# One kernel of a recurrence and a gated layer: constants from one ramp, and a new written order with other banks, queues and engines of copies

## The chip, the core and the metric

The kernel runs on one core of one Trainium2 chip. A core has TensorE (PE in the profile; its weight loads are PEld), VectorE (DVE), ScalarE (ACT) and GpSimd (POOL), which compute, and SyncE (SP), which here only issues transfers. ScalarE and GpSimd can issue transfers too, between their computing instructions. All transfers run on the core's 16 DMA engines. The metric is the device time of one execution in microseconds.

## The reference

A recurrence over 768 steps for 4 batches and 8 heads of 48 channels, and behind it a layer on its 3072 rows of 384:

```python
state = np.zeros((B, H, D, D))
for t in range(S):
    cur = np.einsum('bhd,bhe->bhde', u[None] * kt, vt)
    y[:, :, t] = np.einsum('bhd,bhde->bhe', rt, state + cur)
    state = wt[:, :, :, None] * state + np.einsum('bhd,bhe->bhde', kt, vt)
...
h = x @ w_in                                  # 384 x 1024
sm = e / (np.sum(e, axis=-1, keepdims=True) + 1e-09)      # e = exp(h - max h)
solu = h * sm
ln = (solu - mu) / np.sqrt(var + 1e-06) * g_ln
return (ln @ w_out).astype(np.float32)        # 1024 x 384
```

r, k, v, w, u are the attention inputs (w lies between 0.8 and 0.95), all float32; x is y with its heads side by side.

## The kernel before

The 768 steps are cut into 6 chunks of 128, and a chunk of one batch is a *unit*: 24 units, number 4 times the chunk plus the batch. A unit goes through these stages; the short names are those of the code's table `stages`, and a number behind one is the unit.

- LW, LK, LR, LV load w, k, r and v (192 KB each, into rings of seven buffers).
- lw takes the logarithm of w (ScalarE); cum sums it over the steps with two triangular matrices, `uti_neg` and `uts` (TensorE, 384 columns each); ex is the exponential of the sums, in place in PSUM (ScalarE); kp multiplies by k and r (VectorE) and thereby empties two PSUM banks.
- krk and krr transpose k and r on TensorE, kr copies the result out of PSUM (ScalarE or VectorE). For some units kt does all this with one transposing transfer by SP.
- M is the matrix of scores, m its masked copy (VectorE multiplies with a triangular 0/1 matrix, `keep`).
- p and q are products k r u (GpSimd), dg their sum (VectorE), dv that sum times v (GpSimd): the bonus of the current step. vb is v in bf16 (ScalarE or GpSimd).
- Y is the attention output; y copies it out. Either VectorE adds dv in that copy (the word Y ends in n), or TensorE adds it first with an identity matmul of 384 columns (i) and ScalarE copies.
- S, et, st carry the state on; et is an exponential of 8 columns, st VectorE's update. S uses `halves` and `off_blocks` to set the entries between different heads to exp(-30000).
- X and xT transpose y; H is the product with w_in (24 matmuls of 128 columns into two banks); e its exponential, he the product h e (VectorE), hq its square; Oa and Ob are the two halves of the product with w_out (386 columns), together with one- and two-column matmuls that sum e, he and hq over the row. ea adds the two halves of e beforehand (GpSimd), so that four matmuls sum e and not eight.
- qm, lv, rs make the scale of the row from those sums (VectorE, ScalarE, ScalarE), o scales, out stores.

The softmax sum and the mean cancel out of the layer norm except for these sums, so that no row is divided before the end. Units 17 to 20 make H with rows as the output and turn he by a transfer (ht). Unit 23 is done in two halves (HA, HB and so on).

The weights are prepared once: LI loads w_in in three parts, wi casts them; LO loads w_out in two halves, gw multiplies its eight blocks by the gain, mn forms their column mean (TensorE), mc copies it (ScalarE), ce subtracts it from each block. hot is a number of matmuls of zeros. u and g are spread with us and gs.

The order is written out by hand as a text of words, `ORDER`. A word is a stage with its unit, and behind a point the PSUM bank, or the engine or queue: a for ScalarE, d VectorE, p GpSimd, g GpSimd's queue; a load or store with nothing there is issued by SP. Each engine executes its words strictly in this order (the class `InOrder`, through which every instruction goes: that is why nearly all rows of the profile carry line 86), and the transfers of SP and ScalarE are put in the order of the words too. So a transfer that ScalarE issues stands in its queue between two computing words, and a word that waits holds up all later words of its engine. The first lines, those around the first products with w_in, and the end:

```
hot10.0 LK3.a LW3 LR3.g LW0.a LR0.a lw3 cum3.0 hot2.2 LU0 LW2 LK0.a LG0 lw0 LR2.g cum0.2 ex3 us0.4 LV0.a LW4 LK2
lw2 lw4 kp3 gs0.5 ex0 LR4.g LK4 kp0 cum4.0 ih0 LV4.g ik0 LV2.g LV3.g LR6.g cum2.6 LW1.a uc0 p0 ex2 ex4 krk0.2 kp2
...
st2 Y4.i5 st3 X1.0 lw7 LW9 xT2.a et5 y3.a st4 y4.a lw8 LK8 m5.d mn0.2 X3.4 xT1.d q5 cum7.0 xT3.a st5 ex7 p7 X4.5
H0.6 lw10 mc0 ce7.p ce0.d e0 ce4.d LK10 ce6.d kp7 H1.3 LR8 ce2.d lw9 LW11 e1 he0 ce3.d LV11.g ce5.p H3.0 qh5
...
EB23 out19 DA23 Ob21 QA23.a DB23 qm21 Ob22 lv21 rs21 QB23.d o21.a qm22 out20 out21 lv22 rs22 o22.d out22 Oa23.5
Ob23 qm23 lv23 rs23 o23.a out23
```

The constants (`uti_neg`, `uts`, `ident_f`, `ident`, and later `halves`, `off_blocks`, `keep` by the words ih and ik) are made by GpSimd with memsets and affine selects, sixteen instructions in all.

Of the kernel before, what the change touches and what calls it, by code (L numbers as in the profile page):

```python
# [21 lines left out]
hot10.0 LK3.a LW3 LR3.g LW0.a LR0.a lw3 cum3.0 hot2.2 LU0 LW2 LK0.a LG0 lw0 LR2.g cum0.2 ex3 us0.4 LV0.a LW4 LK2  # L22
lw2 lw4 kp3 gs0.5 ex0 LR4.g LK4 kp0 cum4.0 ih0 LV4.g ik0 LV2.g LV3.g LR6.g cum2.6 LW1.a uc0 p0 ex2 ex4 krk0.2 kp2
krr0 krk3.4 LK1.a LW6 krk2.3 vb0.a krr2 LR5.g kr0.d kr2.a kp4 LK6 krr3 hot1.2 kr3.d M0.1 M3.3 m0.d LR1.a lw6 S0.0
LV1.a m3.d p2 q0 lw1 gc0 LW5 cum6.6 ex6 M2.1 cum1.4 krk4.3 LI0.a krr4 LK5 dg0 m2.d vb3.a kp6 vb2.a lw5 et0 ex1
st0 LO1 vb4.a kp1 cum5.6 hot1.0 q2 LV5.g p3 p1 dv0 ex5 krk1.4 q3 Y0.i5 q1 krr1 dg2 dv2 vb1.a krk6.0 S1.1 LO0.a
kp5 p5 p4 krr6 y0.a kr4.a dg3 krk5.5 dg1 dv1 q4 krr5 kr6.d kr1.a kr5.d et1 Y2.i6 hot1.0 y2.a vb5.a st1 LI2.a M1.2
S3.0 dv3 m1.d wi0.a M4.6 LW7 X0.1 xT0.d S2.5 gw7.a m4.d dg4 LV6.g et3 X2.4 p6 gw4.a LI1.a Y1.n1 LR7.g dv4 LR11.g
y1.d gw2.a gw5.a S4.2 LW10 M6.6 et2 et4 gw0.a S5.3 gw3.a LW8 wi2.p wi1.p gw1.a gw6.a LK7 Y3.i1 q6 m6.d M5.6 LR10
st2 Y4.i5 st3 X1.0 lw7 LW9 xT2.a et5 y3.a st4 y4.a lw8 LK8 m5.d mn0.2 X3.4 xT1.d q5 cum7.0 xT3.a st5 ex7 p7 X4.5  # L30
H0.6 lw10 mc0 ce7.p ce0.d e0 ce4.d LK10 ce6.d kp7 H1.3 LR8 ce2.d lw9 LW11 e1 he0 ce3.d LV11.g ce5.p H3.0 qh5
xT4.d ce1.d LK9 H2.6 hq0.a he1 e3 he3 LW12 e2 krk7.5 Oa0.2 he2 krr7 hq1.a cum10.3 LV8.g Ob0 ex10 Oa1.0 LR9 hq3.a
LV7 p8 cum8.6 LW13 Ob1 LW14 LK11 ex8 q7 vb6.p dg5 kr7.d kp10 lw11 qm0 Oa3.5 lv0 qm1 lv1 LV10.g p10 q8 rs0 M7.3
dg7 rs1 dv5 o0.a out0 vb7.p kp8 lw12 hq2.a Ob3 cum11.6 krk10.2 o1.d H4.0 m7.d Y5.n4 LR12.g dv7 Oa2.3 krr10 qm3
out1 p9 dg6 dg8 ex11 vb8.a dv6 q9 kp11 lv3 cum9.6 e4 rs3 Ob2 y5.d LV9 o3.a he4 ex9 kp9 lw14 kr10.a S7.5 LK12
Y6.n1 qm2 y6.d lv2 krk8.4 Y7.n0 krk11.6 krr8 y7.d S8.7 X5.2 et7 st7 krr11 lw13 rs2 LW17 o2.a et8 cum12.0 LR14.g
xT5.a ex12 q10 kr8.d S6.5 kr11.d hq4.a krk9.2 vb11.p out3 LK14 out2 M8.3 LK13 LR15.g LR17.g krr9 st8 kp12 LK17
et6 kr9.d H5.6 X6.0 m8.a M10.1 st6 e5 xT6.d M9.3 p11 Oa4.5 m10.d LW15 he5 q11 LR13.g X7.0 kt12 cum14.1 m9.a xT7.a
dv8 M11.3 ex14 m11.d sel8 Ob4 vb9.p kp14 LK15 hq5.a cum13.6 LW18 lw17 qm4 S11.0 ex13 Oa5.4 sel9 lv4 lw15 cum17.1
dg9 rs4 LR18.g kp13 Y8.n3 Ob5 ex17 cum15.6 y8.d dv9 o4.a Y9.n3 out4 LV12.g kp17 LV15.g et11 qm5 kt14 S9.5 st11  # L40
ex15 lv5 vb10.a y9.d H6.1 rs5 et9 LV14.g o5.a e6 st9 LV13.g kp15 p12 p13 dg11 he6 dg10 X8.3 X9.0 xT8.a H7.4 out5
q12 xT9.a e7 lw18 hq6.a H8.6 dv11 e8 M12.0 LV16.g he7 H9.2 m12.d LK18 Oa6.5 he8 dg12 e9 vb12.a S10.4 kt15 he9
hq7.a Ob6 hq8.a dv10 LW16 qm6 lv6 rs6 p14 LR16.g et10 Y11.n1 S12.0 et12 Oa7.6 o6.a LK16 y11.d lw16 Y10.n7 st10
Ob7 kt13 y10.d M14.3 st12 vb15.a LK20 M15.1 q13 vb13.a hq9.a qm7 m14.d m15.d lv7 dv12 rs7 Y12.n5 o7.a Oa8.0 y12.d
cum16.3 X11.7 Ob8 cum18.1 out6 p15 ex16 X12.5 xT11.d q14 q15 LR19.g qm8 kp16 vb16.a lv8 H11.6 rs8 o8.a ex18
xT12.d H12.4 LR20.g LW21 vb14.p dg13 LW19 dg15 e11 Oa9.0 p16 kp18 out7 e12 X10.1 dv15 he11 Ob9 xT10.a ea11.p he12
q16 lw21 hq11.a out8 qm9 lv9 M13.1 S15.3 et15 rs9 m13.d ea12.p cum21.4 ex21 o9.d H10.6 LK21 LR21 LW20 Oa11.0
LV18.g st15 kp21 lw19 cum19.1 e10 Ob11 Y15.n4 he10 hq12.a LK19 p18 kt16 S13.3 dv13 Y13.n5 S16.6 qm11 ex19 y15.d
# [52 lines left out]
def kernel(  # L101
# [14 lines left out]
    C = 128  # L116
# [551 lines left out]
```

## Time and profile before

| | |
|---|---|
| three runs | 150.04, 149.55, 146.75 us; median 149.55 |
| the profiled execution | 147.21 us, of which 143.9 are its span |
| mean granted TensorE clock | 0.975 of full speed |
| busy share of the span | PE 90%, VectorE 88%, ScalarE 83%, GpSimd 82% |
| read from HBM, written | 22.03 MB, 4.72 MB |

The page divides the span into 40 slices and gives each engine's busy share in tenths. Groups of instructions stand as line, engine, operation, output and inputs, shapes and count, then their busy time and the mean of one in ns, then the idle time ahead of them and what ended it. In rows in order of time the first number is the start, the second the length, both in us; in square brackets stands the idle time of the engine just before, with what ended it. The mean of a matmul is its way through the array; how fast matmuls follow one another is read from the difference of starts.

### The profile page before, as it was taken

How to read it: one execution, taken by the hardware profiler on the slowest of the kernel's cores; microseconds unless marked ns; L12 is line 12 of the kernel's file. 1: busy time of each engine (PE TensorE's matmuls, PEld its weight loads, DVE VectorE, ACT ScalarE, POOL GpSimd, SP SyncE). 2: the span in 40 equal slices, each digit the busy share in tenths (PEclk: the TensorE clock that was granted, in tenths of full speed). 3: DMA queues.
4: the chain of work that ended last, by engine and by line, in shares of the span. 5: the costliest groups of instructions: out<-in, count | busy, mean ns of one | idle time of the engine just before them, and what ended most of it. 6: DMA issues, size and time to landing. Idle time of an engine off the chain costs nothing.

```text
span 143.9 us, 4779 instructions
## 1 busy us (share of the span) xinstructions
PE 129.1 (90%) x1883; PEld 96.4 (67%) x1883; DVE 126.3 (88%) x218; ACT 119.0 (83%) x241; POOL 117.7 (82%) x151
## 2 busy tenths in 40 slices
PE   6958749869599999999999999999999999999980
PEld 2326418657586778868988787779787565776750
DVE  6028998995899999999999999999999999989760
ACT  3547786989769999999998999959997979967762
POOL 7999959999999989978999999989996997433000
PEclk9995986999999999999999999999999999999999
DMA  4999999999998799999999999999999979443312
GB/s 95 276 287 323 272 310 356 365 348 261 179 267 185 133 245 247 240 201 178 256 225 257 239 262 222 194 280 228 199 199 226 204 170 140 116 107 118 135 55 109
DMA packets 89927, 31.33 MB, mean 218 GB/s; under 512 B 83833, under 2 KB 87938, under 8 KB 89906
## 3 DMA queue, kind: packets, MB, share of 16 engines
q1 hardware_dynamic: 77474, 20.43, 66.2%
q0 software_dynamic: 2112, 6.49, 16.2%
q10 hardware_dynamic: 10320, 4.13, 10.2%
q8 instruction: 14, 0.23, 0.6%
q14 instruction: 7, 0.06, 0.1%
HBM read 22.03 MB, written 4.72 MB: 186 GB/s over the span
## 4 chain that ended last, share of the span: by engine, by line
PE 56%; DMA 20%; DVE 11%; ACT 7%; issue 3%; DVEq 0%; ACTq 0%
PE ps L86 56%; DMA w_in<-in_w_dram 6%; DMA v_in<-in_v_dram 5%; DMA wout_f<-in_moe_w_out_dram 4%; DMA kr_in<-in_k_dram 4%; DVE kp L86 3%; DVE he L86 2%; DVE m L86 2%; ACT w L86 1%; DVE w L86 1%; ACT ps L86 1%; ACT lw L86 1%; DVE dg L86 1%; ACT o L86 1%; DVE y L86 1%
## 5 line engine op out<-in xcount | busy, mean ns | idle before, releaser
L86 PE MATMUL ps<-w,he 128*128 128x386 bf16 x192 | 43.7, 324 | 0.1
L86 PE MATMUL ps<-xT,win_sb 128*128 128x128 bf16 x480 | 29.8, 219 | 1.7 <-DVE kp L86 1.5
L86 PEld LDWEIGHTS <-win_sb 128*128 128x128 bf16 x480 | 27.4, 98 | 3.1 <-DVE kp L86 1.7
L86 DVE TENSOR_TENSOR kp<-ps,kr_in 128x768 bf16<-128x768 f32 x24 | 22.8, 949 | 7.3 <-DMA kr_in<-in_r_dram 4.2
L86 DVE TENSOR_TENSOR m<-ps,keep 128x1024 bf16<-128x1024 f32 x22 | 26.4, 1213 | 0.0
L86 PE MATMUL ps<-one_col,hq 128*128 128x1 bf16 x160 | 26.1, 163 | 0.1
L86 POOL TENSOR_TENSOR p<-kr_in 128x384 bf16<-128x384 f32 x24 | 24.1, 1009 | 1.9 <-DMA kr_in<-in_r_dram 1.7
L86 POOL TENSOR_TENSOR dv<-vb,dg 128x384 bf16<-128x384 bf16 x24 | 20.0, 833 | 6.6 <-DVE dg L86 6.5
L86 DVE TENSOR_TENSOR he<-ps,e 128x1024 bf16<-128x1024 f32 (+1 forms) x21 | 24.1, 1163 | 0.8 <-ACT e L86 0.8
L86 ACT ACTIVATE e<-ps 128x1024 bf16<-128x1024 f32 (+1 forms) x25 | 24.3, 989 | 0.2
L86 ACT ACTIVATE hq<-he 128x1024 bf16<-128x1024 bf16 (+1 forms) x20 | 20.5, 1033 | 2.3 <-DVE he L86 2.3
L86 POOL TENSOR_TENSOR q<-p,u_bc 128x384 bf16<-128x384 bf16 x24 | 21.7, 916 | 0.4 <-DVE dg L86 0.2
L86 PEld LDWEIGHTS <-he 128*128 128x128 bf16 x192 | 18.2, 96 | 3.8
L86 ACT ACTIVATE ps<-ps 128x768 f32<-128x768 f32 x24 | 19.1, 800 | 1.0 <-PE ps L86 0.7
L86 PEld LDWEIGHTS <-hq 128*128 128x128 bf16 x160 | 13.7, 96 | 8.5 <-ACT hq L86 0.3
L86 ACT ACTIVATE lw<-w_in 128x384 bf16<-128x384 f32 x24 | 12.4, 522 | 6.8 <-DMA w_in<-in_w_dram 6.8
L86 POOL DMA_DIRECT2D v_in<-in_v_dram x17 | 15.5, 912 | 0.0
L86 PEld LDWEIGHTS <-kp 128*128 128x128 bf16 x176 | 12.3, 105 | 4.3 <-DVE kp L86 2.7
L86 POOL DMA_DIRECT2D kr_in<-in_r_dram x16 | 14.7, 921 | 0.0
L86 PEld LDWEIGHTS <-kr 64*128 64x128 bf16 (+1 forms) x272 | 10.4, 95 | 6.1 <-issue 2.5
L86 PE MATMUL ps<-signs,e 128*128 128x2 bf16 x88 | 14.5, 165 | 0.0
L86 POOL TENSOR_TENSOR ea<-e 128x512 bf16<-128x512 bf16 x9 | 10.4, 1154 | 5.0 <-ACT e L86 5.0
(94 smaller groups left out, 281.1 us busy)
## 6 DMA issues: line engine op xcount, KB each, us to landing
out_dram<-o SPq DMA_DIRECT2D x24, 192.0 KB, 3.3
w_in<-in_w_dram SPq DMA_DIRECT2D x22, 192.0 KB, 4.7
kr_in<-in_k_dram SPq DMA_DIRECT2D x21, 192.0 KB, 4.5
v_in<-in_v_dram POOLq DMA_DIRECT2D x17, 192.0 KB, 4.8
kr_in<-in_r_dram POOLq DMA_DIRECT2D x16, 192.0 KB, 4.7
win_f<-in_moe_w_in_dram ACTq DMA_DIRECT2D x3, 512.0 KB, 6.6
kr_in<-in_r_dram SPq DMA_DIRECT2D x6, 192.0 KB, 3.9
v_in<-in_v_dram SPq DMA_DIRECT2D x5, 192.0 KB, 6.1
```

What stands on the lines that cost most here:

```text
L86: made = make(*args, **kwargs)
```

## The change

Constants: GpSimd makes one ramp (column minus row) and VectorE compares it with zero for the triangles and the identity; `halves` and `off_blocks` are made by VectorE memsets, with the two rows that count at partitions 0 and 64 instead of 0 and 1. `keep` had the same entries as `uts`, which now masks the scores.

```diff
+    ramp = consts.tile([C, C], BF16)
+    pool.iota(ramp, pattern=[[1, C]], base=0, channel_multiplier=-1, allow_small_or_imprecise_dtypes=True)
     uti_neg = consts.tile([C, C], BF16)
-    pool.memset(uti_neg, -1.0)
-    pool.affine_select(out=uti_neg, in_=uti_neg, compare_op=ALU.is_ge, fill=0.0, base=0,
-                       pattern=[[1, C]], channel_multiplier=-1)
+    dve.tensor_scalar(out=uti_neg, in0=ramp, scalar1=0.0, scalar2=-1.0, op0=ALU.is_ge, op1=MULT)
     uts = consts.tile([C, C], BF16)
-    pool.memset(uts, 1.0)
...
+    dve.tensor_scalar(out=uts, in0=ramp, scalar1=0.0, scalar2=None, op0=ALU.is_gt)
...
+    dve.tensor_scalar(out=ident, in0=ramp, scalar1=0.0, scalar2=None, op0=ALU.is_equal)
...
+    for a in range(2):
+        row = slice(64 * a, 64 * a + 1)
+        dve.memset(halves[row, 64 * a:64 * a + 64], 1.0)
+        dve.memset(off_blocks[row, :, 1 - a:2 - a], -30000.0)
...
-                           in1=keep.unsqueeze(1).to_broadcast([C, H, C]))
+                           in1=uts.unsqueeze(1).to_broadcast([C, H, C]))
```

`ORDER` is replaced as a whole. The new lines in the places shown above:

```
LW3 LW0.a LR3.g LU0 LR0.a hot6.0 LW4 LG0 LK0.g LW2 hot1.0 hot7.0 LK3.g LK4 LR2.g hot4.1 lw3 LK2.g lw0 LW1.a
cum3.4 LW5 us0.1 LR4.g ex3 cum0.6 ex0 LV2.g gs0.0 lw4 LV0.a kp0 p0 uc0 LW6 gc0 hot1.0 LK1.g kp3 cum4.6 krk0.2 lw2
...
et5 y2.a p5 M6.2 st5 LV11 y3.a LK7.a m6.d LW10 gw6.a LV7.a X3.0 dv4 M5.6 gw5.a X1.4 X2.1 gw4.d q5 gw7.a S4.5 m5.d
Y4.i3 wi0.a wi1.p LV6 mn0.2 xT3.a xT2.d LW13 lw7 LW11.a LK10.g wi2.d et4 cum7.0 xT1.d mc0 H0.6 st4 LW8.g ex7
ce7.d LK11 LR10.g y4.a kp7 H1.4 e0 ce1.p ce3.d vb7.d lw10 LK8.a ce2.p H3.0 he0 LV8 e1 LK9.a p6 ce4.d hq0.a H2.6
...
out20 Oa22.6 QA23.a qm21 DB23 lv21 Oa23.0 rs21 o21.a QB23.d out21.a Ob22 Ob23 qm22 lv22 rs22 o22.a qm23 lv23
out22 rs23 o23.a out23.a
```

What the words add up to, where it differs:

| | before | after |
|---|---|---|
| loads of w, k, r, v by SP, ScalarE, GpSimd | 54, 9, 33 | 32, 31, 33 |
| loads of the weights by SP, ScalarE | 1, 4 | 2, 3 |
| stores by SP, ScalarE | 24, 0 | 17, 7 |
| copies of y by VectorE, ScalarE | 20, 4 | 14, 10 |
| copies of kr by VectorE, ScalarE; by transfer | 8, 4; 12 | 4, 7; 13 |
| casts of v by VectorE, ScalarE, GpSimd | 0, 15, 9 | 4, 9, 11 |
| copies of xT by VectorE, ScalarE | 11, 12 | 9, 14 |
| scalings o by VectorE, ScalarE | 6, 18 | 7, 17 |
| units with ea on GpSimd | 9 | 5 |
| casts of w_in by VectorE, ScalarE, GpSimd | 0, 1, 2 | 1, 1, 1 |
| gains of w_out by VectorE, ScalarE, GpSimd | 0, 8, 0 | 1, 6, 1 |
| centrings of w_out by VectorE, GpSimd | 6, 2 | 4, 4 |
| warm-up matmuls in all; ahead of the first cum | 15; 10 | 19; 18 |

The weights' loads come as LI0, LO1, LO0, LI2, LI1 before, and as LO0, LO1, LI2, LI1, LI0 after. Which loads go to which queue differs for more than half of the units; y moves to ScalarE for units 1, 5, 6, 8, 16 and 21, kr for units 3, 5 and 6, and unit 11's k and r are turned by a transfer. ea goes for units 10, 11, 13 and 14. v is cast by VectorE for units 0, 4, 7 and 8. Nearly every bank number differs.

More of the change, by code (lines that the diff above doesn't have):

```diff
@@ L5 @@
 from concourse import mybir
-from concourse.masks import make_identity
 from concourse._compat import with_exitstack
@@ L27 @@
[L27 to L36, printed above, removed]
@@ L206 @@
             dve.memset(kp_t[j][:, :, :, D:], 0.0)
+    ident = consts.tile([C, C], BF16)
+    dve.tensor_scalar(out=ident, in0=ramp, scalar1=0.0, scalar2=None, op0=ALU.is_equal)
+    ident_f = consts.tile([KF, KF], F32)
+    dve.tensor_scalar(out=ident_f, in0=ramp[:KF, :KF], scalar1=0.0, scalar2=None, op0=ALU.is_equal)
+    halves = consts.tile([C, C], BF16)
+    dve.memset(halves, 0.0)
+    off_blocks = consts.tile([C, HP, 2], BF16)
+    dve.memset(off_blocks, 0.0)
+    for a in range(2):
+        row = slice(64 * a, 64 * a + 1)
+        dve.memset(halves[row, 64 * a:64 * a + 64], 1.0)
+        dve.memset(off_blocks[row, :, 1 - a:2 - a], -30000.0)
     mean_w = consts.tile([128, 128], BF16)
@@ L296, in turn_g @@
         ps["g"] = bank([128, KF], F32, x, "g_ps")
-        pe.transpose(ps["g"], g_rows, ident_f[:KF, :KF])
+        pe.transpose(ps["g"], g_rows, ident_f)
     def copy_g(i, x):
```

97 lines of the change are left out of this document (37 added, 60 removed).

## The prediction

> **What bounds the kernel now.** I read the page first, then the busy time of each engine by stage, then the order of time around the two borders that the stages showed.
>
> ```profile
> span 143.9 us, 4779 instructions
> ...
> PE 129.1 (90%) x1883; PEld 96.4 (67%) x1883; DVE 126.3 (88%) x218; ACT 119.0 (83%) x241; POOL 117.7 (82%) x151
> ...
> PE   6958749869599999999999999999999999999980
> ...
> DVE  6028998995899999999999999999999999989760
> ```
>
> Two regimes stand in the slices of 3.6 us. From the twelfth slice on PE and DVE are both full. Before that PE has holes, and DVE has few after the third slice. The table by stage gives the borders; its columns are length, then busy time of PE, weight loads, DVE, ACT and POOL, then granted clock, DMA share, GB/s.
>
> ```profile
> 0.00:10.80 10.80, 7.78 (x23) 3.09 (x23) 3.13 (x24) 4.79 (x8) 9.53 (x27) 0.99 0.97 219
> 10.80:34.30 23.50, 18.14 (x249) 12.93 (x248) 22.17 (x31) 19.10 (x41) 21.71 (x25) 0.86 1.15 324
> 34.30:39.03 4.73, 3.21 (x54) 2.84 (x51) 2.60 (x6) 4.36 (x8) 4.71 (x7) 1.00 0.93 203
> 39.03:133.80 94.77, 94.26 (x1487) 73.63 (x1488) 93.77 (x149) 85.34 (x171) 81.71 (x95) 1.00 0.95 205
> 133.80:143.90 10.10, 5.74 (x77) 3.93 (x74) 4.60 (x10) 5.45 (x16) 0.00 (x0) 0.99 0.26 98
> ```
>
> The long stage, 94.77 us, is closed: PE is busy for 94.26 of it at full clock. A change there can win about 0.5 us unless it takes matmuls away. So gains must come from the 39 us ahead of it, where DVE (22.17 of 23.50) carries the chain, and from the 4.73 us between, where neither PE nor DVE is full. These rows, in order of time, are that border:
>
> ```profile
> 7.33 0.96 DVE L86 TENSOR_TENSOR kp<-ps,kr_in 128x768 bf16<-128x768 f32 x1 [4.23 <-DMA kr_in<-in_r_dram]
> ...
> 9.56 0.52 ACT L86 ACTIVATE lw<-w_in 128x384 bf16<-128x384 f32 x1 [1.96 <-DMA w_in<-in_w_dram]
> ...
> 10.82 0.96 DVE L86 TENSOR_TENSOR kp<-ps,kr_in 128x768 bf16<-128x768 f32 x1 [2.53 <-ACT ps L86]
> ...
> 32.62 2.03 POOL L86 CAST win_sb<-win_f 128x1024 bf16<-128x1024 f32 x2
> ...
> 34.49 3.02 PE L86 MATMUL ps<-xT,win_sb 128*128 128x128 bf16 x48
> ...
> 36.44 1.67 DVE L86 SCALAR_TENSOR_TENSOR w<-wout_f,gr,ps 128x384 bf16<-128x384 f32 x3 [2.13 <-ACT mean_sb L86]
> ...
> 38.02 0.95 DVE L86 TENSOR_TENSOR kp<-ps,kr_in 128x768 bf16<-128x768 f32 x1
> ...
> 39.03 3.15 PE L86 MATMUL ps<-xT,win_sb 128*128 128x128 bf16 x48 [1.52 <-DVE kp L86]
> ```
>
> H0 and H1 start at 34.49, when GpSimd has cast two thirds of w_in. H3 must wait for kp7 to empty its banks, kp7 stands behind three centrings of w_out, and those waited 2.13 us for ScalarE to copy the column mean.
>
> **The change, part by part.** *The start.* GpSimd's sixteen small constant instructions become one iota and ten short VectorE ones. In the trace of before VectorE's first real work is at 7.33, so those lie in its idle time; the cover is over 2 us deep. GpSimd's first load was at 2.69 and can now go up to 1.9 us earlier. Against that, 18 warm-up matmuls stand ahead of the first cumulation where 10 stood.
>
> ```profile
> 1.65 4.05 PE L86 MATMUL ps<-warm 128*128 128x512 bf16 x9
> ...
> 2.69 2.81 POOL L86 DMA_DIRECT2D kr_in<-in_r_dram  x3
> ...
> 6.13 1.06 PE L86 MATMUL ps<-warm 128*128 128x512 bf16 x2
> 6.38 0.80 ACT L86 ACTIVATE ps<-ps 128x768 f32<-128x768 f32 x1 [0.35 <-PE ps L86]
> ```
>
> Nine took 4.05 us, so eight more cost up to 3.6 us, and half of that once the clock is up (the 384-column matmuls further down pass in 0.16 us, where 512 columns take 0.45 here). Nearest to the mixture is 2.5 us: the first cumulation at about 8.0 instead of 5.5. Unit 3's exponential follows, then unit 0's (0.80 us each), since the wait at 9.56 for unit 4's w no longer stands between them. First kp at about 10.1, second at about 11.0, both done near 12.0; before, the second ended at 11.78. So the start gives +0.2 us (from -1.7, if the earlier loads carry the whole chain, to +1.5).
>
> *VectorE's chain to H0.* Durations, for the pieces that change engine:
>
> ```profile
> L86 DVE TENSOR_TENSOR y<-ps,dv 128x384 bf16<-128x384 f32 x20 | 10.9, 548 | 0.5 <-PE ps L86 0.4
> L86 DVE COPY kr<-ps 128x1024 bf16<-128x1024 bf16 x8 | 5.3, 680 | 0.6 <-PE ps L86 0.6
> L86 ACT COPY kr<-ps 128x1024 bf16<-128x1024 bf16 x4 | 4.0, 1016 | 0.9 <-PE ps L86 0.9
> L86 ACT CAST y<-ps 128x384 bf16<-128x384 f32 x4 | 1.9, 494 | 0.0
> L86 ACT CAST vb<-v_in 128x384 bf16<-128x384 f32 x15 | 7.4, 508 | 1.4 <-DMA v_in<-in_v_dram 1.4
> L86 POOL TENSOR_TENSOR ea<-e 128x512 bf16<-128x512 bf16 x9 | 10.4, 1154 | 5.0 <-ACT e L86 5.0
> L86 DVE SCALAR_TENSOR_TENSOR w<-wout_f,gr,ps 128x384 bf16<-128x384 f32 x6 | 3.5, 608 | 2.1 <-ACT mean_sb L86 2.1
> L86 POOL TENSOR_TENSOR w<-w,mean_sb 128x384 bf16<-128x384 bf16 x2 | 1.7, 838 | 0.0
> ```
>
> VectorE loses three kr copies (3 x 0.68) and one y (0.55): -2.6. It gains two casts of v, a gain of w_out and the cast of w_in's third part. None of these stands in the trace on VectorE; bounded by 0.35 and 0.68 for the small ones and by 0.7 and 1.2 for the 1024-wide one, I take 0.45 three times and 1.0: +2.4. Net -0.2. ScalarE gets three kr (3.0) and one y (0.5) and loses two casts of v (1.0) and two gains of w_out (1.2, if one is as long as a centring): +1.3, in a stage where it has 4.4 idle. GpSimd casts one part of w_in instead of two (-1.0), takes one gain (0.8, like its centring) and issues 14 loads ahead of H0 instead of 12 (2 x 0.94), against the constants that it no longer makes. The third w_in part now needs 1.0 us on three engines side by side, not 2.03 on one, so H0 hangs on VectorE's chain and on the mean product. One state update (st4, a 384-wide piece like y's 0.55) stands behind H0 now: 34.5 + 0.2 - 0.2 - 0.5 = 34.0.
>
> *The border.* Between the mean product and its copy ScalarE has an x copy, a logarithm and a short exponential, no longer an 0.8 us one; and VectorE has w_in's cast, two x copies and st4 to do in the 2.13 us in which it waited. Ahead of kp7 stands one centring, not three: 34.0 + 0.5 + 0.6 + 0.95 = 36.1. H3 then follows H1 directly, at 34.0 + 2.7 = 36.7 (two of the 24-matmul products, 1.36 us each by the spacing of 0.06 in the row below), not at 39.03: -2.3 us, the start and the chain included. That is the value I take; it is 0 if kp7 comes where it came, and -4.7 if the whole gap goes.
>
> *The long stage.* Spacing of PE's starts, in the thick of it:
>
> ```profile
> 60.77 0.17 PE L86 MATMUL ps<-signs,e 128*128 128x2 bf16 x1
> 60.80 0.16 PE L86 MATMUL ps<-one_col,hq 128*128 128x1 bf16 x1
> ...
> 63.55 0.32 PE L86 MATMUL ps<-st,ident 128*128 128x384 bf16 x1
> 63.71 0.33 PE L86 MATMUL ps<-vb,kp 128*128 128x96 bf16 x4
> ...
> 67.47 1.50 PE L86 MATMUL ps<-xT,win_sb 128*128 128x128 bf16 x24
> ```
>
> Five y copies of this stage go from VectorE to ScalarE, and the bonus term is then added by a 384-column matmul: 5 x 0.16 = +0.8. Four units lose GpSimd's sum of halves and need eight signed matmuls instead of four: 16 x 0.03 = +0.5. Unit 11's k and r are turned by a DMA: eight matmuls of 0.06 fewer, -0.5. PE: +0.8, all of it on the path. VectorE is relieved of about 3 us here (5 y and one kr are 3.4, two x copies go, a cast and an output scaling come), GpSimd of 4 x 1.15 less three casts; with PE full at 94.26 of 94.77 this can buy back up to 0.5, and I count 0.3.
>
> ScalarE is the doubtful one. Its work grows by 1.4 us (five y at 0.49, three casts of v at 0.51 fewer, two more x copies less one output scaling at about the same length). It had 13 DMA issues, all ahead of H0; now it has 41, of which some 24 lie in the long stage, each in its queue between two computing instructions.
>
> ```profile
> 16.15 0.52 ACT L86 ACTIVATE lw<-w_in 128x384 bf16<-128x384 f32 x1 [0.99 <-DMA w_in<-in_w_dram]
> 16.16 0.37 ACTq L86 DMA_DIRECT2D v_in<-in_v_dram  x1
> ...
> 16.58 0.52 ACT L86 ACTIVATE lw<-w_in 128x384 bf16<-128x384 f32 x1
> ...
> 40.00:130.00 90.00, 89.49 (x1438) 69.99 (x1436) 89.20 (x142) 82.89 (x166) 79.59 (x93) 1.00 0.97 208
> ```
>
> The issue of 0.37 us ran under the logarithm ahead of it, and the next instruction started after 0.43. By the written order all but one of the 24 follow an instruction of 0.4 us or more, so the value is +0.3 for the few exposed; the other end is 24 x 0.37 = 8.9 us, plus waits for a buffer or a store's data, behind which every later ScalarE word stands (exponentials, squares, the row scales). Buffers are freed 17 words or more ahead of their loads; store 2 waits for VectorE's scaling 96 words earlier.
>
> SP, which computes nothing, has 22 loads and seven stores fewer in front of its transposes; a gain there is bounded by PE's idle 0.5 us: 0. GpSimd issues 33 loads as before: 0. Banks: 0, either sign within the 0.5 us of PE's idle time.
>
> *The tail.* o22 moves to ScalarE ahead of unit 23's logarithm:
>
> ```profile
> 139.71 0.29 DVE L86 TENSOR_SCALAR qm<-ps 128x1 f32<-128x1 f32 x1
> 140.03 0.20 ACT L86 ACTIVATE lv<-qm 128x1 f32<-128x1 f32 x1 [1.10 <-DVE qm L86]
> ```
>
> The 1.10 us idle there hides most of a scaling of 0.6 behind two short instructions: +0.2.
>
> Sum: -2.3 (H3's start) - 0.4 (the earlier loads, at a quarter of their best) + 0.8 - 0.3 + 0.3 + 0.2 = -1.7: 145.5 us against the profiled execution's own 147.2 (143.9 of span and 3.3 around). The median of the three runs, 149.55, is 2.3 above that and the fastest, 146.75, 0.5 below; I forecast like against like and keep that spread for the upper end.
>
> A rule speaks against this change. The Trainium skill, "SBUF — State Buffer", section "Who interferes with whom": VectorE and GpSimd share a port pair, and a VectorE cast or tensor_scalar from SBUF to SBUF can hold it, so that GpSimd blocks, its descriptor writing too. No row of before shows such an instruction beside GpSimd; by the rule the first gain would be gone, as in the third rival.
>
> **The rivals.** *More than that (142.3 us).* The loads that start earlier carry the chain: the idle 1.33 us of VectorE between 10.8 and 34.3 goes as well, the start gives -1.2 instead of +0.2, and PE gets the last 0.5: 3.2 us on top. For it: the two waits at 7.33 and 9.56 were for loads. Against: 18 warm-ups.
>
> *ScalarE becomes the bound (151.4 us).* It has 7.1 us idle between 40 and 130, less 1.4 of added copies: 5.7. With the 24 issues unhidden (8.9) it is 3.2 over, PE's 0.8 and the tail's 0.2 come on top, and nothing is won at the border, where ScalarE is busy 4.36 of 4.73. It decides from 0.24 us per issue. Against it: the hidden issue at 16.16.
>
> *No gain ahead of the long stage (148.2 us).* VectorE's new casts read SBUF on both sides; held against GpSimd for their own time (3 x 0.5 + 1.0) they delay p, q and dv, which GpSimd, busy 21.71 of 23.50, can't catch up, and the products that wait for these come no earlier. Or the queues change nothing, as transfers share the same engines at 324 GB/s. Then +0.8, -0.3, +0.3 and +0.2 are left. The Trainium skill's port rule would make it this case; I give that a third of its chance.
>
> **How the numbers follow.** Forecast 0.42, more than that 0.24, ScalarE 0.20, no gain 0.14. The forecast's own range is 143.5 to 147.2; its lower two fifths gain over 2%, about what a measurement of this kernel can tell from no change. Faster: 0.24 + 0.17 = 0.41. Within: 0.25 + 0.14 = 0.39. Slower: 0.20. The range 142.0 to 150.5 leaves out a third of the first rival and half of the second.
>
> **What would show it.** The first kp near 10 and H3 near 36.5 to 37 with no wait for kp; VectorE's idle time up by some 3 us between 40 and 130 with PE still full. If ScalarE's idle time there falls under 2 us and PE waits for its exponentials, the second rival holds. If the idle time ahead of the first centring stays near 2 us, the border was misread. A first kp after 11 would make the start wrong.

## The result and the profile after

| | before | after |
|---|---|---|
| median (lowest to highest) | 148.15 us (146.65 to 150.04), 4 runs | 155.57 us (153.96 to 157.07), 4 runs |
| after by before | | 1.0525, 95% interval 1.0395 to 1.0655 |
| the profiled execution, its span | 147.21, 143.9 us | 153.96, 152.3 us |

The change makes the kernel 5% slower; 145.5 was forecast, and 155.57 lies above the forecast's range, which ended at 150.5. Medians here take all executions, while ratios and their intervals leave the disturbed ones out, so the two can differ by one or two per cent.

The page of the profile after, the lines that answer to those of before (busy time and slices of an engine, 3.8 us a slice):

```profile
span 152.3 us, 4785 instructions
...
PE 132.6 (87%) x1898; PEld 98.8 (65%) x1901; DVE 125.3 (82%) x221; ACT 120.5 (79%) x243; POOL 113.4 (74%) x136
...
PE   6956676598999999999996929999999999999980
...
DVE  7034997779999999999989248899999999988850
```

Two things are new: a hole in the long stage (slices 22 to 24: PE 6, 9, 2, with VectorE at 9, 2, 4), and a head in which VectorE stands at 7 where it stood at 9. The busy time by stage of the kernel after, columns as in the prediction:

```profile
0.00:10.80 10.80, 8.28 (x25) 3.12 (x26) 3.62 (x34) 4.41 (x7) 9.48 (x15) 1.00 0.95 239
10.80:34.30 23.50, 15.99 (x211) 11.91 (x210) 18.26 (x26) 17.80 (x35) 19.00 (x22) 0.78 0.94 274
...
40.00:80.00 40.00, 39.82 (x665) 32.30 (x663) 39.48 (x61) 37.80 (x70) 38.08 (x46) 1.00 1.11 221
80.00:92.00 12.00, 7.41 (x118) 5.95 (x117) 7.15 (x12) 7.18 (x18) 8.93 (x11) 0.98 1.16 238
92.00:130.00 38.00, 37.90 (x581) 28.16 (x581) 36.20 (x55) 32.73 (x69) 28.34 (x35) 0.96 0.94 172
40.00:130.00 90.00, 85.12 (x1358) 66.41 (x1358) 82.84 (x127) 77.71 (x156) 75.36 (x91) 0.98 1.04 202
```

Between 40 and 130 PE idles for 4.88 us where it idled for 0.51, and 4.59 of that lie between 80 and 92. In the head, 10.8 to 34.3, VectorE does 3.9 us less work in the same time (22.17 before) at a lower DMA rate (274 against 324 GB/s): it is waiting, as the rows of the head below show. The starts of the same instructions in both traces, in us, show where the 8.4 us of span come from:

| start of | he1 | he4 | he6 | kp16 | he11 | he14 | he20 | o23 |
|---|---|---|---|---|---|---|---|---|
| before | 41.85 | 52.79 | 70.25 | 82.50 | 85.52 | 105.15 | 124.81 | 140.50 |
| after | 43.01 | 53.90 | 71.86 | 89.53 | 92.19 | 113.15 | 133.41 | 148.89 |
| difference | 1.2 | 1.1 | 1.6 | 7.0 | 6.7 | 8.0 | 8.6 | 8.4 |

*The hole.* The chain of waits of the kernel after, around it (start, length, what):

```profile
71.97 7.48 DMA kr<-kp
79.45 0.02 issue
79.47 9.99 DMA kr_in<-in_r_dram
...
89.53 0.97 DVE kp L85
...
90.55 2.50 PE ps L85 x28
```

VectorE stands at kp16 until the r of unit 16 is there, and TensorE at a product with w_in whose banks kp16 must empty. This load, LR16, went out at 79.47 from ScalarE's queue and took 10 us. Before, GpSimd issued it at 75.97 and kp16 did not wait:

```profile
75.97 0.92 POOL L86 DMA_DIRECT2D kr_in<-in_r_dram  x1
...
82.50 0.96 DVE L86 TENSOR_TENSOR kp<-ps,kr_in 128x768 bf16<-128x768 f32 x1
```

In the chain after, the row ahead of the load is unit 15's transposing transfer. It has no data in common with the load, but it stands eight places ahead of it in the sequence of SP's and ScalarE's transfers; its landing at 79.45 let the load go out 0.02 us later. In the traces these transfers take eight semaphores in turn, and where the landing can be told, none leaves before the one eight places ahead of it has landed.

LR16 is not the whole hole. TensorE's two waits in it, and one of ScalarE:

```profile
81.10 0.52 ACT L85 ACTIVATE lw<-w_in 128x384 bf16<-128x384 f32 x1 [1.03 <-DMA w_in<-in_w_dram]
...
83.31 0.32 PE L85 MATMUL ps<-w,he 128*128 128x386 bf16 x1 [1.25 <-ACT xT L85]
...
90.55 1.80 PE L85 MATMUL ps<-xT,win_sb 128*128 128x128 bf16 x24 [3.21 <-DVE kp L85]
```

Of the 4.59 us idle, 3.21 are the wait for kp16. In the other 1.25 TensorE waits for a copy of xT, which stands on ScalarE behind lw19, and that waited for the w of unit 19: GpSimd issued it at 72.67, and it landed 8.4 us later.

What was issued around it, in the kernel after, and how the transfers issued between 71 and 86 us fared there (KB each, median us to landing):

```profile
71.97 1.24 SPq L85 DMA_TRANSPOSE kr<-kp  x1
...
73.88 5.07 SPq L85 DMA_TRANSPOSE kr<-kp  x1
...
79.47 0.38 ACTq L85 DMA_DIRECT2D kr_in<-in_r_dram  x1
```

```profile
w_in<-in_w_dram POOLq DMA_DIRECT2D x3, 192.0 KB, 8.4
...
out_dram<-o SPq DMA_DIRECT2D x2, 192.0 KB, 9.5
v_in<-in_v_dram SPq DMA_DIRECT2D x2, 192.0 KB, 8.1
...
kr<-kp SPq DMA_TRANSPOSE x2, 11.0
```

In the same stretch of before the four loads of w took a median of 4.3 us and the three stores 4.2.

*Its echo.* After the hole the granted clock (the number ahead of the last two) is low, in the table by windows of the kernel after:

```profile
90.50:93.00 2.50, 2.45 (x31) 2.11 (x32) 2.50 (x4) 0.61 (x1) 0.68 (x1) 0.72 1.13 205
93.00:96.00 3.00, 3.00 (x42) 2.10 (x39) 2.06 (x3) 1.91 (x5) 2.49 (x3) 0.66 1.14 254
96.00:100.00 4.00, 4.00 (x72) 3.23 (x67) 3.77 (x6) 3.86 (x8) 3.92 (x5) 1.00 1.25 180
```

5.5 us at about 0.7 are 1.7 us of TensorE's time lost on top of the hole (2.5 x 0.28 + 3.0 x 0.34). Some 1.4 of them fall behind the start of he11 (3.81 us from 92.19 to 96 at 0.63), about the further 1.3 us between he11 and he14. The Trainium skill, "TensorE: Matmul & The Clock Gate", section "HAM oscillation — how this bites in real kernels", has a wait for a load throttle the array so; these rows, after a wait of 3.21 us, agree.

*The head.* VectorE's rows of the kernel after that waited for loads, and the chain of waits behind the second:

```profile
10.23 1.82 DVE L85 TENSOR_TENSOR kp<-ps,kr_in 128x768 bf16<-128x768 f32 x2 [6.09 <-ACT ps L85]
...
15.36 0.36 DVE L85 CAST vb<-v_in 128x384 bf16<-128x384 f32 x1 [1.52 <-DMA v_in<-in_v_dram]
...
27.34 0.96 DVE L85 TENSOR_TENSOR kp<-ps,kr_in 128x768 bf16<-128x768 f32 x1 [1.50 <-DMA kr_in<-in_k_dram]
```

```profile
20.39 0.41 ACT lw L85
20.80 0.00 ACT y L85
20.81 6.41 DMA kr_in<-in_k_dram
...
27.34 0.97 DVE kp L85
...
28.36 2.69 PE ps L85 x34
```

The k of unit 5 was issued by SP at 15.60 before; now ScalarE issues it, behind its copy y0, at 20.81. It takes 6.4 us, and kp5, at 22.10 before, starts at 27.34. The first product with w_in starts at 37.90 (34.49 before). The two waits for loads, 3.0 us, are most of the 3.9 us by which VectorE's idle time in the head grew; the rest are short waits for TensorE and ScalarE. From H0 on the border is quick, as forecast: four products follow one another without a break.

### The profile page after: what moved, and what is told of

Its sections match the earlier page's. It is cut to its first block, busy times and chain, and to the rows that moved or that the text cites. A ratio compares the mean times of both kernels' runs of the same rounds, so it can differ in the third digit from the quotient of the medians.

```text
span 152.3 us, 4785 instructions
## 1 busy us (share of the span) xinstructions
PE 132.6 (87%) x1898; PEld 98.8 (65%) x1901; DVE 125.3 (82%) x221; ACT 120.5 (79%) x243; POOL 113.4 (74%) x136
## 3 DMA queue, kind: packets, MB, share of 16 engines
q10 hardware_dynamic: 34064, 9.31, 27.3%
## 4 chain that ended last, share of the span: by engine, by line
PE 51%; DMA 16%; POOL 14%; DVE 10%; ACT 4%; issue 3%; ACTq 0%; DVEq 0%; POOLq 0%
PE ps L85 50%; DMA kr_in<-in_r_dram 7%; DMA kr<-kp 5%; DMA kr_in<-in_k_dram 4%; DVE kp L85 4%; POOL kr_in L85 3%; DVE m L85 2%; POOL q L85 2%; POOL w_in L85 2%; POOL dv L85 2%; POOL w L85 2%; POOL p L85 2%; DVE st L85 1%; ACT ps L85 1%; ACT lw L85 1%
## 5 line engine op out<-in xcount | busy, mean ns | idle before, releaser
L85 PE MATMUL ps<-w,he 128*128 128x386 bf16 x192 | 44.6, 329 | 1.3 <-ACT xT L85 1.2
L85 PEld LDWEIGHTS <-win_sb 128*128 128x128 bf16 x480 | 27.9, 98 | 4.8 <-DVE kp L85 3.4
L85 DVE TENSOR_TENSOR m<-ps,uts 128x1024 bf16<-128x1024 f32 x22 | 26.8, 1216 | 1.6 <-PE ps L85 1.6
L85 PEld LDWEIGHTS <-hq 128*128 128x128 bf16 x160 | 14.7, 97 | 9.9 <-issue 0.9
L85 PE MATMUL ps<-signs,e 128*128 128x2 bf16 x120 | 19.9, 166 | 0.0
L85 PEld LDWEIGHTS <-kp 128*128 128x128 bf16 x168 | 11.7, 105 | 5.8 <-DVE kp L85 3.5
L85 PEld LDWEIGHTS <-kr 64*128 64x128 bf16 (+1 forms) x272 | 10.9, 98 | 6.0 <-issue 3.3
L85 POOL TENSOR_TENSOR ea<-e 128x512 bf16<-128x512 bf16 x5 | 5.8, 1153 | 10.5 <-ACT e L85 10.5
L85 PEld LDWEIGHTS <-e 128*128 128x128 bf16 x120 | 11.7, 97 | 2.0 <-issue 1.6
L85 DVE TENSOR_TENSOR st<-ps,et 128x384 bf16<-128x384 f32 x20 | 10.9, 549 | 2.1 <-ACT et L85 1.9
```

Of the source, the lines that this page charges most:

```text
L85: made = make(*args, **kwargs)
```

## The experiments

Theory Q: the new places of the loads (which queue, behind which words) cost the time. Rival O: the new order of the computing words does. Rival C: the constants do. The first three kernels separate these; the next ones follow single loads. "Before" beside each is the kernel before, run with it. Where an expectation says "erf", it means the exponential e of the layer.

**Constants alone.** The order and queues of before, with the constants of the change.

```diff
-cum4.0 ih0 LV4.g ik0 LV2.g LV3.g LR6.g
+cum4.0 LV4.g LV2.g LV3.g LR6.g
+    ramp = consts.tile([C, C], BF16)
...
```

> The old order and queues with the new constants alone (the ramp by GpSimd, the compares and memsets by VectorE, uts as the mask; the words ih and ik go). If the constants have a part in the loss, 150 us or more (half of the loss of some 7.5 us or more). My theory is that they have none: VectorE's constants end near 4.2 us in the changed kernel, and its first kp needs nothing before 7; so within 1.5 us of the kernel before, 146 to 149, and the span's first GpSimd load near 1.4 instead of 2.7.

Measured: 150.66 us (148.86 to 153.14) beside 148.51; ratio 1.0144, interval 1.0027 to 1.0261. So the constants have a part in the loss, against the theory: 1.4% of the change's 5.3, with an interval from 0.3 to 2.6. In the profiled execution (153.14, the longest of the four) lw4 waited 4.2 us for its w, which SP issued and which landed 8.0 us after its issue instead of 5.5, while GpSimd's own earlier loads landed after a median of 4.9 us, as before. I read this as GpSimd's loads taking the transfer time of SP's.

**Old queues under the new order.** Each load and store of the changed kernel goes back to the queue that it had before; the order of words stays.

```diff
-LW3 LW0.a LR3.g LU0 LR0.a hot6.0 LW4 LG0 LK0.g
+LW3 LW0.a LR3.g LU0 LR0.a hot6.0 LW4 LG0 LK0.a
...
-hq8.a LR16.a q13
+hq8.a LR16.g q13
```

> The changed kernel with every load and store back on the queue it had before, at its new place in the order. Theory Q (the loads on ScalarE's queue are the loss: they go out late and their packets run beside the transposing transfers): the idle 3.65 us ahead of unit 16's kp goes, and the time falls by 5 us or more, to 147 to 150.5. Theory O (the written order itself, with its banks and copies, is the loss): within 2 us of the changed kernel, 153 to 157.

Measured: 158.36 (156.12 to 160.09) beside 148.51; ratio 1.0578 (1.0460 to 1.0697). Slower still than the change, which neither theory had. Its waits for loads (in all, times, longest):

```profile
ACT lw L83 <- DMA w_in<-in_w_dram: 6.6, 3, 3.4
DVE kp L83 <- DMA kr_in<-in_k_dram: 6.3, 2, 5.9
```

The hole is still there: kp16 waits 3.13 us, now for its exponential, which stands on ScalarE behind the longest of these waits for w.

**New queues under the old order.** The reverse: before, with each load and store on the queue of the change.

```diff
-hot10.0 LK3.a LW3 LR3.g LW0.a LR0.a
+hot10.0 LK3.g LW3 LR3.g LW0.a LR0.a
...
```

> The old order, banks, copies and constants, with the new queues alone. Theory Q: slower than before by 3 us or more, 151 to 157, with ScalarE or VectorE idle until a load lands somewhere after 60 us. Theory O: within 1.5 us of before, 146 to 149.5.

Measured: 161.89 (159.51 to 164.82); ratio 1.0835 (1.0691 to 1.0980), with 10.9 us of waits for w alone. So theory Q falls in this form: putting the queues back mends nothing. Rival O, by which the old order keeps its time on any queues, falls too: the new queues under it are worse than either order with the queues written for it. An order and its queues fit each other, which points to the places of single loads; the next runs move these.

**Unit 16's r earlier.** One word of the changed kernel moves.

```diff
-p12 LK17.a LK18 cum13.6
+p12 LK17.a LR16.a LK18 cum13.6
...
-hq8.a LR16.a q13
+hq8.a q13
```

> The changed kernel with one word moved: the load of unit 16's r, still by ScalarE, stands behind unit 17's k (near 64 us) and no longer behind unit 8's square (79.5 us). If that one late load is what the long stage lost, unit 16's kp starts near 85 instead of 89.5 and the time falls by 3 to 5 us, to 150 to 152.5. If the queues as a whole are short (every landing from 72 to 86 us took 7 to 11 us), another wait for a load takes its place and the time stays above 153.5.

Measured: 151.55 (150.19 to 154.76) beside 148.51. One load costs 4.0 of the 7.4 us that the medians of the result differ by. TensorE still idles for 1.94 us ahead of 84.02, for the copy of xT behind the w of unit 19, for which lw19 now waits 2.49. The row of kp16, without a wait:

```profile
86.51 0.95 DVE L83 TENSOR_TENSOR kp<-ps,kr_in 128x768 bf16<-128x768 f32 x1
```

**Unit 5's k earlier, too.**

```diff
-p1 y0.a LK5.a st0
+p1 y0.a st0
...
-ex2 LR1.a kr0.d
+ex2 LR1.a LK5.a kr0.d
```

> The kernel with unit 16's earlier load (151.55), and one word more moved: the second half of unit 5's k, on ScalarE's queue behind y0, is issued right behind the load LR1 instead. Theory H, this late load is the head's loss: it is issued near 13 instead of 20.8, lands by 21, the multiply kp5 starts by 26.0 instead of 27.5 with no wait of over 0.5 us for k, the first erf result of each of units 0 to 4 comes 1.0 to 1.5 us earlier, and the time is 150.0 to 150.6. Rival, the head is bound by the order of VectorE's and ScalarE's work or by the transfers' rate: kp5's wait goes or shrinks but another wait takes its place (for v or for another k), the erfs of units 0 to 4 stay within 0.4 us, and the time stays 151.2 to 152.

Measured: 155.62 (153.57 to 156.39) beside 148.95; ratio 1.0353 (1.0218 to 1.0488). Slower than without the edit, which neither theory had. kp5 lost its wait (26.76), but in the profiled execution (156.39, the longest of the four) this stands ahead of he0, VectorE's rows first, GpSimd's second:

```profile
38.47 3.29 DVE L83 CAST vb<-v_in 128x384 bf16<-128x384 f32 x1
41.68 1.20 DVE L83 TENSOR_TENSOR he<-ps,e 128x1024 bf16<-128x1024 f32 x1
```

```profile
37.28 1.63 POOL L83 TENSOR_TENSOR w<-w,mean_sb 128x384 bf16<-128x384 bf16 x2
38.86 1.00 POOL L83 TENSOR_TENSOR p<-kr_in 128x384 bf16<-128x384 f32 x1
39.82 0.90 POOL L83 TENSOR_TENSOR w<-w,mean_sb 128x384 bf16<-128x384 bf16 x1
40.67 0.93 POOL L83 DMA_DIRECT2D kr_in<-in_r_dram  x1
41.62 0.86 POOL L83 TENSOR_TENSOR w<-w,mean_sb 128x384 bf16<-128x384 bf16 x1
```

The cast of unit 7's v, 0.53 us in the kernel after, takes 3.29: it ends about when a load's descriptors, written behind GpSimd's tensor operations, end, near 41.6. That is what a later expectation calls theory L: the cast from SBUF to SBUF waits for GpSimd. It is read from these ends, not shown. The rule weighed in the prediction (the Trainium skill, "SBUF — State Buffer", section "Who interferes with whom") names such a pair, and that whoever comes first blocks the other; here VectorE would be the one blocked, but the section has the pair held for one instruction, and this cast lasts over several.

The cast is not where most of the 4 us go. Beside the run before, he0 is 0.6 us later (41.68, then 41.08), so that the cast took back what the earlier k had won. kp16 is 4.1 us later (90.61, then 86.51): behind he0 loads are late again, the w of unit 19 by 3.2 us.

**And unit 0's v earlier.**

```diff
-lw4 LV0.a kp0
+lw4 kp0
...
-lw0 LW1.a cum3.4
+lw0 LW1.a LV0.a cum3.4
```

> As the run with unit 5's earlier k, and unit 0's second half of v is issued right behind LW1 on ScalarE's queue instead of behind the first decay exponentials. Theory H (a late load each time): the cast vb0 loses its 1.52 us wait, VectorE starts what follows it a us earlier, the erfs of units 0 to 4 come another 0.5 to 1.0 us earlier, and the time is 149.2 to 150. Rival, the transfers' rate is spent: what lands earlier for unit 0 lands later for unit 4 or 5, the erfs of units 0 to 4 stay within 0.4 us of the run before, and so does the time.

Measured: 151.58 (151.17 to 152.22); ratio 1.0132 (1.0042 to 1.0222). Little of it is the v: vb0 still waited 1.34 us, as the earlier load took 9.9 us. The same cast began at 38.90 and took 1.40, ending 0.2 us after GpSimd's operation of 39.18 to 40.08. he0 comes 1.5 us earlier than in the run before, kp16 5.7: most of the gain lies behind he0 again.

**That cast on GpSimd.** Unit 5's and unit 16's loads earlier, and one letter.

```diff
-ce3.d vb7.d lw10
+ce3.d vb7.p lw10
```

> The kernel with unit 5's earlier k (155.62, of which 2.9 us are a cast of unit 7's v on VectorE that took 3.29 us instead of 0.5 and stood just ahead of the first multiply he0), with that one cast on GpSimd instead. Theory L, the cast of SBUF to SBUF waits until GpSimd's run of tensor operations ends: without it he0 starts near 39 instead of 41.7, the erfs of units 0 to 4 come 1.5 to 2.5 us earlier than in the kernel with unit 16's earlier load, and the time is 149.5 to 152. Rival, the 3.29 us are of one profiled run only, and that kernel is slow for its transfers (unit 19's w 3.2 us late): he0 near 39 to 40, and the time stays 154 or longer.

Measured: 150.21 (148.15 to 154.19, 10 runs) beside 149.18; ratio 1.0116 (1.0056 to 1.0177), against 1.0353 with the cast on VectorE: 2.4% for one letter, the intervals apart. That is not the price of the cast: by the medians the two differ by 5.4 us, and the first multiply of the layer starts only 2.7 us earlier, of which 0.9 are there at kp5. With v0 early too and the cast still on VectorE (1.40 us) the ratio was 1.0132, no different from 1.0116. The rows:

```profile
25.86 0.95 DVE L83 TENSOR_TENSOR kp<-ps,kr_in 128x768 bf16<-128x768 f32 x1
...
38.94 1.23 DVE L83 TENSOR_TENSOR he<-ps,e 128x1024 bf16<-128x1024 f32 x1
```

**The cast on GpSimd, unit 5's k late.** This divides the head between the two; only unit 16's load is early.

> The kernel with unit 16's earlier load (151.55) with the cast of unit 7's v on GpSimd instead of VectorE, and unit 5's k as late as the change has it. There this cast took 0.48 us, as its width asks, so theory L expects little of it: he0 between 40.4 and 41.1, the time 151 to 151.7; then of the 2.1 us that he0 came earlier in the run with both edits, 1.4 to 2.1 are unit 5's k. Rival, the cast on VectorE is the loss by itself and the k load is none: he0 at 39.0 to 39.6, the time 149.5 to 150.3.

Measured: 156.54 (151.57 to 160.47, 4 runs) beside 148.57. Neither range of he0 held. The spread is wide, and the profiled execution is the longest of the four, so I take only the order of events in its head:

```profile
28.21 0.96 DVE L83 TENSOR_TENSOR kp<-ps,kr_in 128x768 bf16<-128x768 f32 x1 [2.83 <-DMA kr_in<-in_k_dram]
...
41.64 1.23 DVE L83 TENSOR_TENSOR he<-ps,e 128x1024 bf16<-128x1024 f32 x1
```

The wait for k is there and he0 is late (41.1 in the kernel with unit 16's load alone), so the cast is not the loss by itself. As far as one profiled execution tells, the 2.1 us by which he0 comes earlier with both edits need the earlier k load, and by the run with that load alone they need the cast on GpSimd too.

**Without three transposing transfers.** The changed kernel without kt13, kt14 and kt15; the scores of these units are made with older transposes, so its output is not the reference's.

```diff
-he6 kt15 X9.0
+he6 X9.0
...
```

> The changed kernel (155.57) without the transposing transfers of units 13, 14 and 15, so the scores of these units are multiplied with older transposes; everything else is issued in the same places. Theory T, a transposing transfer holds up the loads beside it and they its own: the landings issued from 70 to 82 us fall from 7 to 11 us to about 5, LR16 goes out before 79 and lands by 84, the multiply kp16 has no wait of over 1 us, and the time falls by 4 to 5 to 150.5 to 151.5. Rival, the loads of that stretch are too many whatever else runs (about 170 GB/s asked for at its end): landings stay 7 us or longer, kp16 waits 2 us or longer, and the time stays 154.5 to 156. Third, both by half: LR16 still goes out late (the eighth transfer before it, which the transpose was, being replaced by another) but lands in 5 us: 152 to 153.5.

Measured: 150.46 (149.31 to 153.75, 10 runs) beside 148.95, 5.1 below the changed kernel. LR16 goes out at 77.80 and kp16 starts at 84.67 without a wait. Unit 16's r is there 8.4 us earlier (81.08, then 89.46): 1.7 of them are the earlier issue, and 6.7 the way, 3.3 us instead of 10.0. So what the load lost by waiting for the transfer eight places ahead was the smaller part; most was lost on the way, beside the transposes. Between 71 and 86 us, and in the stage of the hole:

```profile
w_in<-in_w_dram POOLq DMA_DIRECT2D x3, 192.0 KB, 5.1
```

```profile
80.00:92.00 12.00, 12.00 (x210) 9.88 (x206) 11.55 (x19) 11.23 (x25) 11.81 (x15) 1.00 0.80 171
```

**The same cut in the kernel before**, as a control: kt13, kt14 and kt15 left out, output likewise not the reference's.

> The kernel before (148.95) without the transposing transfers of units 13, 14 and 15, whose scores are multiplied with older transposes: the control of the same cut in the changed kernel, which took that from 155.57 to 150.46. Theory T, they cost time only where loads stand behind them just in time: here TensorE is full from 39 us on, and the time stays 148 to 149.5. Rival, the three transfers cost any kernel of this kind some time: 144 to 146.

Measured: ratio 0.9984 (0.9931 to 1.0036); the medians are 146.83 (146.00 to 148.71, 10 runs) beside 149.18 (145.60 to 153.88, 23 runs). So these transfers cost nothing in the kernel before, where no engine waits more than 0.4 us for a load in that stretch.

**Ten warm-ups instead of eighteen**, with unit 16's load early.

```diff
-LW2 hot1.0 hot7.0 LK3.g
+LW2 LK3.g
```

> The kernel with unit 16's earlier load (151.55) without 8 of the 18 warm-up matmuls ahead of the first cumulative sum (the two words with one and seven of them). Theory, the head is bound by loads and by VectorE's order, not by the warm-ups: the first sum starts near 5.6 instead of 7.6 or waits there for lw3, the granted clock of the first 25 us stays within 0.03, the erfs of units 0 to 4 come at most 0.6 us earlier, and the time stays 151 to 152. Rival, the warm-ups hold the first sum and with it all of the head: the first kp 1.5 to 2 us earlier, and the erfs of units 0 to 4 with it, time 149.6 to 150.2. Below both, a colder TensorE: later erfs and a time of 152 or longer.

Measured: 151.80 (150.08 to 155.82, 10 runs), ratio 1.0216 (1.0133 to 1.0298): no gain. The first kp starts 1.8 us earlier than in the kernel with unit 16's load alone (9.31), he0 does not (41.52, then 41.08), and kp5 waits again:

```profile
7.52 1.82 DVE L83 TENSOR_TENSOR kp<-ps,kr_in 128x768 bf16<-128x768 f32 x2 [3.37 <-DMA kr_in<-in_k_dram]
...
27.52 0.96 DVE L83 TENSOR_TENSOR kp<-ps,kr_in 128x768 bf16<-128x768 f32 x1 [1.84 <-DMA kr_in<-in_k_dram]
```

**Eight mends together.** To the loads of units 16, 5 and 0 and the cast come four more: two loads change places, and three words move (of these only the new places are shown).

```diff
-ex16 LK19.a q14
+ex16 LK21.a q14
-e12 LK21.a S15.7
+e12 LK19.a S15.7
...
+S9.5 LW16.g LW19.g lv5
+qm6 LR21 kt13 hq9.a
+p17 LV16 LV19 dg14
```

> The kernel with the earlier halves of k of unit 5 and v of unit 0 (151.58), and five words more: the cast of unit 7's v on GpSimd; unit 21's half of k ahead of unit 19's, which is needed later; unit 19's w one place of GpSimd's queue earlier; the transposing transfer of unit 13 behind the r load of unit 21, out of the crowd at 74 to 79; and the v load of unit 19 behind that of unit 16. Theory, the order itself is sound and its late loads are the loss: he0 near 39, kp21 with no wait of over 0.5 us, PE idle under 2 us between 80 and 112 instead of 3, and the time 147 to 149, at the kernel before's or under it. Rival, the transfers of the new order have no slack, and each load put earlier makes another late: a new wait of 1 us or longer at some w, k or v, and the time 150.5 to 152.

Measured: 149.20 (148.79 to 152.83, 6 runs) beside 149.18; ratio 1.0165 (1.0070 to 1.0260). he0 comes at 38.48 and he11 at 85.35, both ahead of the kernel before, and then he14 at 107.42, 2.3 behind it. In between GpSimd waits for a load of v:

```profile
99.67 0.50 POOL L83 CAST vb<-v_in 128x384 bf16<-128x384 f32 x1 [1.65 <-DMA v_in<-in_v_dram]
```

The next two expectations take this cast for vb19 and the moved LV19 for its cause. It is vb18: by the order of GpSimd's words vb19 is the cast before it, at 95.69, without a wait, and the load that landed just ahead of 99.67 is LV18, issued by SP at 94.16.

**LV19 back, unit 15's r earlier.**

```diff
-p17 LV16 LV19 dg14
+p17 LV16 dg14
...
-LR13.g vb11.a
+LR13.g LR15.g vb11.a
```

> The version with eight words mended (149.2), with the v load of unit 19 back at its place (moved later it made GpSimd's cast vb19 wait 1.65 us, and TensorE idle 1.11 us between 104 and 112), and unit 15's r load right behind that of unit 13 on GpSimd's queue (kp15 waited 0.68 us for it). Theory, what is left over the kernel before is these late loads: no wait of VectorE, ScalarE or TensorE for a load of over 0.5 us after 39 us, TensorE idle under 0.6 us between 60 and 112 instead of 2.2, and the time 1.0 to 1.8 less, 147.4 to 148.2. Rival, the order itself has more work on TensorE than the kernel before: TensorE busy throughout and the time still 148.6 or longer.

Measured: 152.34 (150.26 to 156.60, 6 runs) beside 148.57; ratio 1.0247 (1.0108 to 1.0386). Worse, and neither theory holds. TensorE waited 1.68 us at 61.33, and ahead of it GpSimd:

```profile
57.50 1.01 POOL L83 TENSOR_TENSOR p<-kr_in 128x384 bf16<-128x384 f32 x1 [2.91 <-DMA kr_in<-in_r_dram]
```

This is not unit 12's r, which the next expectation names. The product is p8, and the load is LR15 itself, issued at 52.85 and landed at 57.44. The rings hold seven buffers, so unit 15's r goes into the buffer of unit 8's, and the new place of LR15 is ahead of p8. So p8 waits for the new r and multiplies that: this kernel does not compute unit 8's bonus rightly, and it tells nothing of the transfers' slack.

**LV19 back, nothing else.**

> The version with eight words mended (149.2) with the v load of unit 19 back at its place, and nothing else: the r load of unit 15, which put earlier made that of unit 12 late by 2.9 us (152.34), stays where the change has it. Theory, single late loads are the rest: the wait of vb19 and TensorE's 1.11 us idle between 104 and 112 go, and the time is 147.6 to 148.6, within 1% of the kernel before. Rival, this order's transfers have no slack from 40 to 112 us: another load is late by a us or more in its place, and the time 149 to 151.

Measured: 149.52 (146.03 to 151.10, 6 runs) beside 149.09 (146.23 to 154.84), no difference that these runs can tell, and no version that beats the kernel before. Its profiled execution still waited for loads of v, 2.36 us for that of unit 9 at 56.92 and 1.31 for that of unit 18, the wait that the move of LV19 had been blamed for:

```profile
101.07 0.50 POOL L83 CAST vb<-v_in 128x384 bf16<-128x384 f32 x1 [1.31 <-DMA v_in<-in_v_dram]
```

**Constants alone, with unit 4's w first.**

```diff
-LW3 LR3.g LW0.a
+LW3 LW4 LR3.g LW0.a
```

> The kernel with the new constants alone (150.66), with unit 4's w load moved to the second place of SyncE's queue. In that run GpSimd, done with its constants, issues its first eight loads from 1.4 to 7.7 instead of 2.7 to 13.1, and unit 4's w, on SyncE's queue, lands 8.0 us after its issue instead of 5.5: the 4.2 us wait of lw4 holds the first multiplies of units 0, 2 and 4 by 2.5 us. Theory, that collision is all that the constants lose: lw4 waits under 1.5 us, the multiply kp0 is at 10.8 or earlier, and the time is 147.8 to 149. Rival, the early loads take the transfers' rate whatever is first: another load (k0, w2 or v0) is late by as much, and the time stays 150 to 151.5.

Measured: 151.97 (150.77 to 157.29, 5 runs); ratio 1.0337 (1.0196 to 1.0478). The rival's mechanism holds, with a time above its range: in the profiled execution (157.29, the longest of the five) kp and p now wait for k, 4.6 and 5.6 us at the longest.

## Why the prediction was wrong

*The start* was right. First kp near 10.1 and second near 11.0, both done near 12.0: 10.23, 11.14 and 12.05. But it was costed as if an earlier start could be kept. With ten warm-ups kp0 came 1.8 us earlier and he0 not at all: the loads set the head.

*The earlier loads, -0.4*, had the wrong sign. By the run with the constants alone, which is 1.4% slower under the old order, GpSimd's earlier loads came out of SP's and ScalarE's; the page of before has 276 and 287 GB/s in the two slices from 3.6 to 10.8 us, where the load that came late lies.

*VectorE's chain to H0, -0.2, with H0 at 34.0,* is the first step that failed. Its work was summed rightly, and VectorE indeed has less to do, but the chain waited for loads that the sum took as there: 1.52 us for v0 and 1.50 for k5, 3.0 of the 3.9 by which H0, at 37.90, missed the forecast. That many loads changed queue was counted; that LK5 had moved from SP to a place behind y0 on ScalarE was not followed.

*The border* was right in itself: from H0 to H3 in two products instead of 4.54 us. It only started 3.4 us later, so that at he4 the balance was +1.1 and not -2.3.

*The long stage* is the second step that failed, and the larger one. "The long stage, 94.77 us, is closed" took the loads of before for granted; "all but one of the 24 follow an instruction of 0.4 us or more" asked what an issue costs ScalarE, and not what the load loses by standing behind ScalarE's words, behind the transfer eight places ahead, and by running beside other transfers than before. For ScalarE the answer was right: it idles for 12.3 us between 40 and 130, so the second rival is out. For the loads it was 4.6 us of TensorE's time, 3.2 for LR16 and 1.25 behind unit 19's w, which stands on GpSimd's queue, and 1.3 of clock behind them. The gain of 0 for "SP, which computes nothing" missed that SP's transposing transfers share the sequence with ScalarE's loads and run beside them. VectorE's idle time there rose by 6.4 us, but PE was not full beside it.

*TensorE's added work* fits its counts: 120 and 20 matmuls for the sums of e instead of 88 and 36, ten with dv instead of four, eight fewer for kp. *The tail* was right: from he22 to o23 8.73 us against 8.65.

*The third rival* had the place of the head's loss, and the port rule was not needed for it in the changed kernel, where the casts took 0.35 to 0.75 us. If it decided anywhere, it was in the run with unit 5's earlier k.

Left open: the last per cent or two of this order over the kernel before, and the wide spread of some of its versions (151.6 to 160.5 in one). Every version of the new order carries the new constants, and these alone cost 1.4% under the old order, as much as what is left (1.2 to 1.7%); the new order with the old constants was not run, so the constants may be the whole rest. Mending single loads reached the kernel before and no further; whether the order could be freed of late loads altogether was not found. And why unit 15's transpose and the loads beside it took so long is not settled: the run without three transposes shows only that they are needed for it.

## What to carry to other kernels

When a load moves to another queue, follow it from its new place to its first reader: behind which computing words does it stand, which transfers stand ahead of it, and how many microseconds are left. A stage that is "closed" by one engine is closed only as long as its loads arrive; with little slack, an earlier load can be paid for by another one, as in the run with unit 4's w first. A load may also not go ahead of the last reader of its buffer. After each mended wait look for the next, and name its load by the order of words and the time of landing, before counting the gain.

## What was not expected of the hardware

- A transposing transfer can take five times as long beside other traffic, and the other transfers with it. Its 1024 packets of 256 bytes, by the packet records of the traces, take 1.0 us where little else moves (79.15 to 80.18 in the kernel before), up to 3.2 elsewhere in that kernel, and 5.4 in the kernel after (73.18 to 78.53), where 0.36 MB of other queues' packets moved in that time, 67 GB/s. Loads issued between 71 and 86 us landed after 7.1 to 8.4 us in the median instead of 4 to 5; without three transposes it was 3.3 to 5.8.
- In this program a transfer of SP or ScalarE leaves only when the one eight places ahead in their common sequence has landed, whose semaphore it takes: LR16 at 79.47 after kt15's landing at 79.45. With kt13 to kt15 left out the load left at 77.80.
- A VectorE cast of 0.5 us from SBUF to SBUF took 3.29 beside GpSimd's back-to-back work in one profiled execution, and 1.40 in that of another version.
- A wait of 3.2 us of TensorE cost another 1.3 to 1.7 in clock.
